# Row maxima turned pair by pair as seven 16-bit columns, with the bias product cut in four, in an attention and soft-MoE kernel

## The chip, the cores and the metric

The kernel runs on one core of one Trainium2 chip. The time is that of one execution on the device, in microseconds (us). The kernel before has a median of 298.84 us over three runs (298.15 to 299.03).

## The reference, cut to what matters

```python
# q, k, v: (8, 12, 448, 64) float32
scores = q @ k.T / 8
m = max(scores, axis=-1)
e = exp(scores - m)
attn = e / (sum(e, axis=-1) + exp(-m) + 1e-9)
x = (attn @ v), as 3584 rows of 768
logits = x @ phi                       # phi: 768 x 32
d = softmax of logits over the rows;   slot_input = d.T @ x
h = relu(slot_input[e] @ w1[e]);       slot_out[e] = h @ w2[e]     # 8 experts, 768x1024 and 1024x768
out = softmax of logits over the slots @ slot_out
```

## The kernel before, in words

**Pairs.** Two heads make a pair; there are 48 pairs (`NPAIR`), six to a batch element. Head 0 of a pair lies on partitions 0 to 63, head 1 on 64 to 127, so a product over the 64 channels of a head uses half of TensorE's rows, and the two heads' products can run side by side. The 448 queries are four blocks `i` of 128, 128, 128 and 64. For each pair the kernel does the following.

- `T(n)`, line 241: 28 transposes (L256) of 64x64 turn q and k; one copy takes the result from PSUM, on VectorE (L265) for two pairs in three, on ScalarE (L263) for the third. `NQK` = 7 turned pairs are kept.
- `A(n, i)`, line 274: scores of query block `i`, queries on the partitions (L285, L294, L304), into one of three PSUM buffers (`psA`), and VectorE's row maximum (L287, L298, L307). Seven maxima to a pair: two heads for each of the blocks 0 to 2, one for both heads of the half block 3.
- `W1`, `W2`, `W3`, lines 310 to 349: once for three pairs, GpSimd writes the negated maxima into a 128x4x128 tile `wm`, four matmuls turn it (L336, L337) into a row of 448 for each head and pair, ScalarE copies that as `mT` (L342), and two small exponentials give exp(-m) (L345, L348).
- `Bk(n, i)`, line 352: the scores again, keys on the partitions (L367 or L396), and onto them, in PSUM, the bias: the weights are a 0/1 column `sel` spread over the output's columns, the moving operand is `mT`, 448 wide (L370 or L399), one matmul for each head. ScalarE's exponential (L372, L402) reads the sum. Four PSUM buffers (`psB`), which `T`, `W2` and `PX` use too.
- `AV(n, i, qs)`, line 421: the product with v, 24 matmuls of 65 columns with 128-column weights and 8 with 64 columns (L436), into one PSUM buffer (`psV`); `N1` (ScalarE copy, L449) and `N2` (VectorE L464 and L465, GpSimd L469 to L480) divide by the sum; `PX` (L501, copy L507) turns the result.
- `P(b)`, line 516: after each batch element, the soft-MoE logits and their running sums, in steps spread over later half-pairs (`post`).

**The order is written out by hand.** Each engine works off its instructions in the order of the program. A string `ramp` (line 716) gives the order of the first pairs; then a loop (line 758) runs over the pairs `s` = 3 to 48, in two halves `y`. The list `runs` holds all `A(n, i)` in order (`i` = 0, 3, 1, 2 within a pair), and `As(c)` or a mixed `Bk` takes the next one from it. At `s` = 3, 26 of them have been taken: the maxima are (26 - 12)/4 = 3.5 pairs ahead. A half is *mixed* when the next `A` has `i` = 1 - `y` (line 761). A mixed `Bk` with `i` below 3 issues its matmuls as

```python
a0()         # A's head 0
score(1)
score(0)
bias(1)      # with its exponential
bias(0)
a1()         # A's head 1
```

so that the halves of the array hold (a0, score 1), (score 0, bias 1), (bias 0, a1). In the second half the block `i` = 3 of `Bk` follows with the `A` of `i` = 3 between its scores and its biases (`side`).

**Loads** all go out on GpSimd's queue (`load`, `load_part`), but for some of the last weight rows, which wait in DRAM in 16 bits and come by SyncE's queue (`stage_rows`, `fetch_rows`). `V(g)` (line 406, L408 to L411) is GpSimd's copy of v for three pairs, which waits for v's load. In the ramp, `G0` is `V(0)`, the load of v for group 1 and the fill of a buffer; `J0` is the load of q and k of group 2 and of a first weight half in two DMAs; `K0` is `V(1)`.

**The end.** After the last pair come the last `P`, the experts' products (`hidden` L862, `slots` L882) and the output (L925, sent at L941).

Of the kernel before, what the change touches and what calls it, by code (L numbers as in the profile page):

```python
# [8 lines left out]
F32 = mybir.dt.float32  # L9
# [22 lines left out]
def kernel(  # L32
# [39 lines left out]
    sel = const.tile([128, HG], BF16, name="sel")  # L72
    phi_sb = const.tile([128, KC, NS], BF16, name="phi_sb")
    halfm = const.tile([128, 2], F32, name="halfm")
    nhalfm = const.tile([128, 2], F32, name="nhalfm")
# [4 lines left out]
    NQK, NE, VPN, NATV = 7, 5, HG * 4 * VS, HG * 4 * D  # L80
    sizes = [("nq0", 2 * NP * S), ("nq1", 2 * NP * S), ("nv", NATV), ("qk6", 2 * S), ("wm1", 512),
             ("qk0", 2 * S), ("qk1", 2 * S), ("qk2", 2 * S), ("wm0", 512), ("xTa", 4 * 512), ("qk3", 2 * S),
             ("vp0", VPN), ("x0", 4 * DD), ("qk4", 2 * S), ("qk5", 2 * S), ("e2", NE * 2 * S), ("e1", S),
             ("vp1", VPN), ("xTb", 2 * 512), ("x1", 4 * DD)]
# [13 lines left out]
    wm = [part(f"wm{i}", 0, 512).rearrange("p (i c) -> p i c", i=4) for i in range(2)]  # L98
# [57 lines left out]

    with ExitStack() as at:
# [7 lines left out]
        nat = {}  # L165
        ubuf = pu.tile([128, 2, 7 * W65], F32, name="ubuf")
# [30 lines left out]
        for t in wm:  # L197
            nc.vector.memset(t, 0.0)
# [9 lines left out]
        for t, x in ((halfm, 1.0), (nhalfm, -1.0)):  # L208
            nc.vector.memset(t, 0.0)
            for hl in range(2):  # L210
                nc.vector.memset(t[64 - 64 * hl:128 - 64 * hl, hl:hl + 1], x)
# [10 lines left out]
        for base in (0, 64):  # L222

            nc.gpsimd.affine_select(
                out=sel[base:base + 64], in_=sel[base:base + 64], fill=1.0,
                compare_op=ALU.not_equal, base=0,
                pattern=[[-1, HG]], channel_multiplier=1)
# [3 lines left out]
        mx, ngm, ec, mT, eT, av, us = {}, {}, {}, {}, {}, {}, {}  # L231
# [9 lines left out]
        def T(n):  # L241
            g, pl = divmod(n, NP)
            first = n < NP * NP
# [26 lines left out]
        firsts = [0, 1] + list(range(3, NPAIR, 3))  # L270
        group = {n: (m, n - a) for m, (a, z) in enumerate(zip(firsts, firsts[1:] + [NPAIR])) for n in range(a, z)}
        mg, mpl = (lambda n: group[n][0]), (lambda m: (0, (firsts + [NPAIR])[m + 1] - firsts[m]))

        def A(n, i, steps=False):
            g, pl = group[n]
            if g not in mx:
                mx[g] = psm.tile([128, 21], F32, tag="mx", name="mx")
            t = qkT[n]
            if steps:
                m = mx[g]  # L280

                def run(hl):
                    r = slice(64 * hl, 64 * hl + 64)
                    ps = psA.tile([128, 512], F32, tag="a", name="ps_a")
                    nc.tensor.matmul(ps[:, 0:S], t[r, 0, i * 128:(i + 1) * 128], t[r, 1, :], start=True, stop=True)  # L285
                    c = HG * i + 2 * pl + hl
                    nc.vector.reduce_max(m[:, c:c + 1], ps[:, 0:S], axis=AX.X)  # L287

                return [lambda: run(0), lambda: run(1)]
            if i < 3:  # L290
# [5 lines left out]
                for hl in range(2):  # L296
                    c = HG * i + 2 * pl + hl
                    nc.vector.reduce_max(mx[g][:, c:c + 1], pss[hl][:, 0:S], axis=AX.X)  # L298
            else:
# [6 lines left out]
                c = 3 * HG + pl  # L306
                nc.vector.reduce_max(mx[g][:, c:c + 1], ps[:, 0:S], axis=AX.X)  # L307


        def W1(g):  # L310
            w, m = wm[g % 2], mx[g]
            l0, l1 = mpl(g)
            nm = psm.tile([128, 21], BF16, tag="ngm", name="ngm")
            neg = lambda o, s: nc.gpsimd.tensor_scalar(o, s, -1.0, None, op0=ALU.mult)
            cols = lambda t: t[:, 0:3 * HG].rearrange("p (i c) -> p i c", i=3)[:, :, 2 * l0:2 * l1]

            o = w[:, 3, :].rearrange("p (d c) -> p d c", d=2)[:, :, 2 * l0:2 * l1]
            nc.gpsimd.tensor_mul(
                o.rearrange("p d (l h) -> p d l h", h=2),
                m[:, 3 * HG + l0:3 * HG + l1].unsqueeze(1).unsqueeze(3).to_broadcast([128, 2, l1 - l0, 2]),  # L320
                nhalfm.unsqueeze(1).unsqueeze(1).to_broadcast([128, 2, l1 - l0, 2]))
            o = w[:, 0:3, :].rearrange("p i (d c) -> p i d c", d=2)[:, :, :, 2 * l0:2 * l1]
            neg(o, cols(m).unsqueeze(2).to_broadcast([128, 3, 2, 2 * (l1 - l0)]))
            if l1 - l0 == NP:
                neg(nm, m)
            else:
                nc.gpsimd.memset(nm, 0.0)
                neg(cols(nm), cols(m))
                neg(nm[:, 3 * HG + l0:3 * HG + l1], m[:, 3 * HG + l0:3 * HG + l1])
            ngm[g] = nm  # L330

        def W2(g):
            w = wm[g % 2]
            ps = pb_("ps_m")
            for i in range(3):
                nc.tensor.matmul(ps[:, i * 128:(i + 1) * 128], w[:, i, :], ident, start=True, stop=True)  # L336
            nc.tensor.matmul(ps[:, 384:448], w[:, 3, :], ident2[:, 0:64], start=True, stop=True)  # L337
            st["ps_m"] = ps

        def W3(g):  # L340
            t = psm.tile([128, S], BF16, tag="mT", name="mT")
            nc.scalar.copy(t, st["ps_m"][:, 0:S])  # L342
            mT[g] = t
            e = psm.tile([128, NP, 7], F32, tag="ec", name="ec", bufs=3)
            nc.scalar.activation(e[:, :, 0:6].rearrange("p l (i h) -> p i l h", i=3),  # L345
                                 ngm[g][:, 0:18].rearrange("p (i l h) -> p i l h", i=3, h=2),
                                 AF.Exp, scale=scale)
            nc.scalar.activation(e[:, :, 6], ngm[g][:, 18:21], AF.Exp, scale=scale)  # L348
            ec[g] = e


        def Bk(n, i, c=0, mix=False):

            g, pl = group[n]
            t = qkT[n]
            rs = [slice(0, 64), slice(64, 128)]
            if i < 3 and mix and runs and runs[0][1] < 3:
# [7 lines left out]
                def score(hl):  # L365
                    pss[hl] = pb_("ps_b")
                    nc.tensor.matmul(pss[hl][:, 0:S], t[rs[hl], 1, cols], t[rs[hl], 0, :], start=True, stop=False)  # L367

                def bias(hl):
                    nc.tensor.matmul(pss[hl][:, 0:S], sel[rs[hl], 2 * pl + hl:2 * pl + hl + 1].to_broadcast([64, 128]),  # L370
                                     mT[mg(n)][rs[hl], :], start=False, stop=True)
# [6 lines left out]
                bias(1)  # L378
                bias(0)
# [15 lines left out]
            for hl in range(2):  # L395
                nc.tensor.matmul(outs[hl], t[rs[hl], 1, cols], t[rs[hl], 0, :], start=True, stop=False)  # L396
            As(c)
            for hl in range(2):
                nc.tensor.matmul(outs[hl], sel[rs[hl], 2 * pl + hl:2 * pl + hl + 1].to_broadcast([64, m]), mT[mg(n)][rs[hl], :],  # L399
                                 start=False, stop=True)  # L400
# [14 lines left out]
        def av_tile(n):  # L415

            if n >= NPAIR - 3:
                return psA.tile([128, 512], F32, tag="a", name="ps_av")
# [22 lines left out]
        on_pool = lambda n: n < NPAIR - 4  # L441
# [10 lines left out]
        def N2(n):  # L452
# [5 lines left out]
            e = ec[mg(n)][:, group[n][1], :]  # L458
# [220 lines left out]
        for z in range(3):  # L679
            post.setdefault(2 * NPAIR - 5 + 2 * z, []).append(last[z])  # L680


        runs = [(n, i) for n in range(NPAIR) for i in (0, 3, 1, 2)]
# [8 lines left out]
        for _ in range(22):  # L692
            nc.tensor.matmul(ps[:, 0:64], wm[0][:, 0, :], wm[0][:, 0, 0:64], start=True, stop=True)
# [3 lines left out]
        rows_at = {77: 3, 83: 7, 85: 12, 89: 17, 91: 20, 92: 24, 93: 26, 95: 27}  # L697
        rows = 0
        stage_at = {34: [(16, 20), (20, 24)], 37: [(27, 29), (29, 32)], 40: [(32, 36), (36, 40)]}
        wait_loads = []  # L700
        waits = [r for z in stage_at.values() for y in z for r in range(*y)]
        def slot_loads(s):
            g = (s + 10) // 3
            if s == 1 or (s and s % 3 == 2):
# [4 lines left out]
            if s % 3 == 0 and g - 2 < NG - 1:  # L709
# [6 lines left out]
        ramp = ("T0 A A T1 A A W0 T2 A G0 A X0 J0 A B0.0 A B0.1 A A T3 A B0.2 A A T4 C0.3 V0.0 W1 A V0.1 V0.2 A X1 T5 "  # L716
                "A B1.0 A K0 V0.3 H0 C1.1 N0 B1.2 A T6 C1.3 V1.0 V1.1 A B2.0 M0 K1 A T7 B2.1 A V1.2 V1.3 W2 T8 H1 A "
                "N1 B2.2 Y2 V2.0 X2 C2.3 Z0 V2.1 M1 K2 ")
        for word in ramp.split():
# [7 lines left out]
            elif op == "W":  # L727
                W1(*arg)
            elif op == "X":
                W2(*arg)  # L730
                W3(*arg)
# [22 lines left out]
            elif op == "Z":  # L754
                PX(0)
            elif op == "K":
                slot_loads(*arg)
        for s in range(3, NPAIR + 1):
            for y in range(2):
                hs = 2 * s + y  # L760
                mix = len(runs) > 1 and runs[0][1] == 1 - y
# [17 lines left out]
                else:  # L779
                    if s < NPAIR - 6:  # L780
                        T(s + 6)
                    if s and s + 1 in firsts:
                        W2(mg(s + 1))
                        W3(mg(s + 1))
# [7 lines left out]
                if y == 0:  # L792
                    if 0 <= s - 1:
                        for i in range(4):
                            AV(s - 1, i, [3])
                        if s == NPAIR:
                            PX(s - 2)
                        N1(s - 1)
                        if not on_pool(s - 1):
# [4 lines left out]
                if y == 0 and s and s + 1 in firsts:  # L804
                    W1(mg(s + 1))
# [226 lines left out]
```

## Time and profile before

| | |
|---|---|
| median of three runs | 298.84 us (298.15 to 299.03) |
| span of the profiled execution | 298.99 us, printed as 299.0 |
| TensorE (PE) busy | 271.4 us, 91%, 5174 matmuls |
| VectorE (DVE) busy | 249.7 us, 84% |
| ScalarE (ACT) busy | 249.8 us, 84% |
| GpSimd (POOL) busy | 195.9 us, 66% |
| DMA | 58.67 MB, mean 196 GB/s |
| granted TensorE clock | full until the output stage |
| first exponential of pairs 0, 1, 2, 3, 4 | 12.75, 22.34, 27.16, 33.95, 38.62 us |
| first exponential of pairs 43 and 47, last of pair 47 | 229.05, 247.19, 250.1 us |

A line of the profile names the engine, the line of the kernel, the operation and its tiles: `L285 PE MATMUL ps_a<-W` is the matmul of line 285 that writes `ps_a`. PEld is the weight load of a matmul. "64\*128" is the part of the array used, rows by columns; "64x448" is the moving operand. The profiled execution spans 0.15 us more than the median of the runs, and nothing that the page shows lies around the span.

### The profile page before, as it was taken

The page shows a single profiled execution, that of the slowest core. Times are in us where ns is not written, and L with a number is a line of the kernel's source. Part 1 is how long each engine was busy: PE and PEld are TensorE (multiplying, and loading weights), DVE is VectorE, ACT ScalarE, POOL GpSimd, SP SyncE. Part 2 cuts the span into 40 slices and gives each one's busy share as a digit, 9 for nine tenths or more (in the row PEclk, how much of TensorE's full clock was granted, in tenths as well). Part 3 has the DMA queues.
Part 4 walks back from the last instruction along what each step waited for, and adds up shares of the span by engine and source line. Part 5 has one row for each costly group of instructions (what it writes and reads, how often), then busy time and mean ns, then how long its engine had stood idle before and what let it go on. Part 6 is the DMA issues. An engine that isn't in the chain of part 4 may idle for free.

```text
span 299.0 us, 12398 instructions
## 1 busy us (share of the span) xinstructions
PE 271.4 (91%) x5174; PEld 162.5 (54%) x5174; DVE 249.7 (84%) x581; ACT 249.8 (84%) x559; POOL 195.9 (66%) x391
## 2 busy tenths in 40 slices
PE   5999899999999999999899999999999999996820
PEld 4445456566666566566556666656665555652100
DVE  5899799999999989999889999998999675537930
ACT  3569999999899989998989899989999987337820
POOL 8792887979696979887879697978686633000000
PEclk9999999999999999999999999999999999997555
DMA  7999998999999999999999999999799989908997
GB/s 132 147 143 208 149 138 138 188 165 188 185 204 179 184 176 202 163 182 182 202 159 184 176 199 152 196 183 196 125 150 187 213 185 263 344 10 318 380 453 322
DMA packets 47015, 58.67 MB, mean 196 GB/s; under 512 B 2800, under 2 KB 39920, under 8 KB 46704
## 3 DMA queue, kind: packets, MB, share of 16 engines
q0 software_dynamic: 40304, 42.29, 89.6%
q1 hardware_dynamic: 6656, 15.60, 13.8%
q8 instruction: 40, 0.66, 0.8%
q14 instruction: 15, 0.12, 0.1%
HBM read 89.16 MB, written 15.14 MB: 349 GB/s over the span
## 4 chain that ended last, share of the span: by engine, by line
PE 68%; ACT 10%; DVE 6%; POOL 6%; issue 4%; DMA 2%; DVEq 0%; POOLq 0%; ACTq 0%
PE ps_av L436 15%; PE ps_a L285 10%; PE ps_b L367 7%; PE ps_b L370 7%; PE ps_t L256 5%; PE ps_b L396 5%; PE ps_x L501 3%; PE ps_b L399 3%; ACT W L402 2%; PE ps_o L925 2%; DVE mx L298 2%; PE ps_s L623 2%; PE ps_h L862 2%; PE ps_so L882 2%; ACT W L263 2%
## 5 line engine op out<-in xcount | busy, mean ns | idle before, releaser
L287 DVE TENSOR_REDUCE mx<-ps_a 128x1 f32<-128x448 f32 x250 | 137.3, 613 | 4.6 <-PE ps_a L285 3.5
L372 ACT ACTIVATE W<-ps_b 128x448 bf16<-128x448 f32 x250 | 120.4, 574 | 0.0
L285 PE MATMUL ps_a<-W 64*128 64x448 bf16 x250 | 80.9, 352 | 0.0
L367 PE MATMUL ps_b<-W 64*128 64x448 bf16 x250 | 70.5, 352 | 1.1
L436 PE MATMUL ps_av<-W 128*128 128x65 bf16 (+1 forms) x1536 | 64.9, 196 | 2.2 <-issue 1.6
L436 PEld LDWEIGHTS <-W 128*128 128x128 bf16 (+1 forms) x1536 | 50.5, 100 | 30.2 <-issue 26.4
L370 PE MATMUL ps_b<-mT,sel 64*128 64x448 bf16 x250 | 66.5, 350 | 0.0
L469 POOL TENSOR_TENSOR W<-ubuf,rec 128x384 bf16<-128x384 f32 x44 | 36.3, 824 | 35.7 <-ACT W L507 19.3
L402 ACT ACTIVATE W<-ps_b 128x448 bf16<-128x448 f32 x86 | 46.1, 574 | 2.0 <-PE ps_b L399 2.0
L256 PEld LDWEIGHTS <-W 64*64 64x64 bf16 x1344 | 29.3, 112 | 12.7 <-issue 4.3
L507 ACT CAST W<-ps_x 128x512 bf16<-128x512 f32 x47 | 28.6, 608 | 7.4 <-PE ps_x L501 7.2
L256 PE MATMUL ps_t<-ident,W 64*64 64x64 bf16 x1330 | 30.6, 195 | 2.4 <-ACT W L215 1.4
L307 DVE TENSOR_REDUCE mx<-ps_a 128x1 f32<-128x448 f32 x48 | 29.5, 615 | 1.4 <-PE ps_a L304 1.4
L285 PEld LDWEIGHTS <-W 64*128 64x128 bf16 x250 | 23.4, 94 | 9.8
L114 POOL DMA_DIRECT2D W<-in_moe_w_dram x30 | 22.6, 755 | 7.9 <-PE ps_b L399 7.8
L370 PEld LDWEIGHTS <-sel 64*128 64x128 bf16 x250 | 19.6, 94 | 14.4 <-issue 5.6
L396 PE MATMUL ps_b<-W 64*64 64x448 bf16 (+1 forms) x134 | 27.1, 374 | 0.3
L449 ACT COPY ubuf<-ps_av 128x455 f32<-128x455 f32 x44 | 25.1, 571 | 0.8 <-POOL W L408 0.6
L399 PE MATMUL ps_b<-mT,sel 64*64 64x448 bf16 (+1 forms) x134 | 25.1, 354 | 0.1
L263 ACT COPY W<-ps_t 128x896 bf16<-128x896 bf16 x21 | 19.5, 927 | 6.5 <-PE ps_t L256 6.5
L298 DVE TENSOR_REDUCE mx<-ps_a 128x1 f32<-128x448 f32 x38 | 21.1, 616 | 1.9 <-PE ps_a L294 1.9
L480 POOL TENSOR_TENSOR W<-ubuf,rec 128x128 bf16<-128x128 f32 x44 | 17.5, 398 | 3.7
(156 smaller groups left out, 446.6 us busy)
## 6 DMA issues: line engine op xcount, KB each, us to landing
W<-in_moe_w_dram POOLq DMA_DIRECT2D x24, 768.0 KB, 9.9
W<-in_v_dram POOLq DMA_DIRECT2D x32, 192.0 KB, 6.5
out_dram<-W SPq DMA_DIRECT2D x2, 2688.0 KB, 10.0
W<-in_q_dram POOLq DMA_DIRECT2D x15, 336.0 KB, 6.3
W<-in_k_dram POOLq DMA_DIRECT2D x15, 336.0 KB, 7.5
stage<-in_moe_w_dram POOLq DMA_DIRECT2D x4, 768.0 KB, 9.6
W<-stage SPq DMA_DIRECT2D x4, 576.0 KB, 7.3
out_dram<-W SPq DMA_DIRECT2D x6, 384.0 KB, 3.0
```

Of the source, the lines that this page charges most:

```text
L256: nc.tensor.transpose(o, src[r, pl, tok * D:(tok + 1) * D], ident[r, r])
L285: nc.tensor.matmul(ps[:, 0:S], t[r, 0, i * 128:(i + 1) * 128], t[r, 1, :], start=True, stop=True)
L287: nc.vector.reduce_max(m[:, c:c + 1], ps[:, 0:S], axis=AX.X)
L307: nc.vector.reduce_max(mx[g][:, c:c + 1], ps[:, 0:S], axis=AX.X)
L367: nc.tensor.matmul(pss[hl][:, 0:S], t[rs[hl], 1, cols], t[rs[hl], 0, :], start=True, stop=False)
L370: nc.tensor.matmul(pss[hl][:, 0:S], sel[rs[hl], 2 * pl + hl:2 * pl + hl + 1].to_broadcast([64, 128]), mT[mg(n)][rs[hl], :], start=False, s ...
L372: nc.scalar.activation(e[:, hl, :], pss[hl][:, 0:S], AF.Exp, scale=scale)
L396: nc.tensor.matmul(outs[hl], t[rs[hl], 1, cols], t[rs[hl], 0, :], start=True, stop=False)
L399: nc.tensor.matmul(outs[hl], sel[rs[hl], 2 * pl + hl:2 * pl + hl + 1].to_broadcast([64, m]), mT[mg(n)][rs[hl], :], start=False, stop=True)
L402: nc.scalar.activation(e, p[:, 0:S], AF.Exp, scale=scale)
L436: nc.tensor.matmul(o, eT[n, i, hl][:, qc], vp[g % 2][:, 2 * pl + hl, i, 0:W65], start=(i == 0 and u == 0 and hl == 0) or (u == 3 and i == ...
L469: eng.tensor_mul(x[:, 0:3, c:c + 128].rearrange("p i (h d) -> p i h d", h=2), u[:, 0:6, 0:D].rearrange("p (i h) d -> p i h d", h=2), rec[: ...
```

## The change

- The maxima of a pair are written by VectorE directly as seven 16-bit columns of a tile `mxr` (128 x 6 pairs x 64), not negated. `W1` on GpSimd, the tiles `wm`, `ngm` and `nhalfm` go.
- `W2(n)` runs for each pair: two transposes of 128x64 (one for each half of the output's partitions) and one ScalarE copy of 128x128 as `mT`. `EC` is one exponential for up to three pairs.
- `sel` holds -1, seven columns. The bias of a `Bk` is put on in four pieces of 128, 128, 128 and 64 columns for each head (`lower`): another column of `sel` for each piece, so 8 weight loads and 8 matmuls where there were 2 and 2.
- `NQK` = 5; `T` runs 4 pairs ahead in place of 6; the loads of q and k are issued at other places; a piece of the last weights gets room of its own (`own`).
- `runs` takes `i` in the order 0, 1, 3, 2; a half is mixed when the next `A` has `i` = 2 - `y`; the ramp is shorter and the loop begins at `s` = 2. In the ramp `J0` stands ahead of `G0`.

```diff
-    NQK, NE, VPN, NATV = 7, 5, HG * 4 * VS, HG * 4 * D
+    NQK, NE, VPN, NATV = 5, 5, HG * 4 * VS, HG * 4 * D
...
+        def W2(n):
+            ps = psB.tile([128, 128], BF16, tag="b", name="ps_m")
+            for r in rs:
+                nc.tensor.transpose(ps[r, :], mxr[:, n % (2 * NP), :], ident)
+            mT[n] = psm.tile([128, 128], BF16, tag="mT", name="mT", bufs=3)
+            nc.scalar.copy(mT[n], ps)
...
+        def lower(outs, n, m):
+            for i in range(4):
+                for hl, o in outs.items():
+                    c = 2 * i + hl if i < 3 else 6
+                    nc.tensor.matmul(o[:, i * 128:min(i * 128 + 128, S)], sel[rs[hl], c:c + 1].to_broadcast([64, m]),
+                                     mT[n][rs[hl], slice(0, 128) if i < 3 else rs[1 - hl]], start=False, stop=True,
+                                     skip_group_check=True)
...
                 a0()
                 score(1)
                 score(0)
-                bias(1)
-                bias(0)
+                lower({hl: pss[hl][:, 0:S] for hl in (1, 0)}, n, 128)
+                expo(1)
+                expo(0)
                 a1()
...
-            for hl in range(2):
-                nc.tensor.matmul(outs[hl], sel[rs[hl], 2 * pl + hl:2 * pl + hl + 1].to_broadcast([64, m]), mT[mg(n)][rs[hl], :],
-                                 start=False, stop=True)
+            lower(dict(enumerate(outs)), n, m)
...
-        runs = [(n, i) for n in range(NPAIR) for i in (0, 3, 1, 2)]
+        runs = [(n, i) for n in range(NPAIR) for i in (0, 1, 3, 2)]
...
-        ramp = ("T0 A A T1 A A W0 T2 A G0 A X0 J0 A B0.0 A B0.1 A A T3 A B0.2 A A T4 C0.3 V0.0 W1 A V0.1 V0.2 A X1 T5 "
-                "A B1.0 A K0 V0.3 H0 C1.1 N0 B1.2 A T6 C1.3 V1.0 V1.1 A B2.0 M0 K1 A T7 B2.1 A V1.2 V1.3 W2 T8 H1 A "
-                "N1 B2.2 Y2 V2.0 X2 C2.3 Z0 V2.1 M1 K2 ")
+        ramp = ("T0 A A T1 A A T2 A W0 J0 G0 A B0.0 A B0.1 T3 A B0.2 A C0.3 W1 T4 A V0.0 V0.1 A B1.0 V0.2 V0.3 H0 N0 A K0 "
+                "C1.1 T5 A B1.2 W2 A C1.3 E M0 K1 V1.0 V1.1 A Y ")
...
-        for s in range(3, NPAIR + 1):
+        for s in range(2, NPAIR + 1):
             for y in range(2):
                 hs = 2 * s + y
-                mix = len(runs) > 1 and runs[0][1] == 1 - y
+                mix = len(runs) > 1 and runs[0][1] == 2 - y
...
-                    if s < NPAIR - 6:
-                        T(s + 6)
-                    if s and s + 1 in firsts:
-                        W2(mg(s + 1))
-                        W3(mg(s + 1))
+                    if s < NPAIR - 4:
+                        T(s + 4)
...
+                        if s + 1 < NPAIR:
+                            W2(s + 1)
                         N1(s - 1)
+                        if s == 2 or s % 3 == 1 and s < NPAIR:
+                            EC(s - 1, s + 2 - (s == 2))
```

## The prediction

> **What bounds the kernel now.** I read the page's shares first, then the chain of waits, then the timeline of single pairs on each engine, and last GpSimd's queue at the start.
>
> ```profile
> PE 271.4 (91%) x5174; PEld 162.5 (54%) x5174; DVE 249.7 (84%) x581; ACT 249.8 (84%) x559; POOL 195.9 (66%) x391
> PE 68%; ACT 10%; DVE 6%; POOL 6%; issue 4%; DMA 2%; DVEq 0%; POOLq 0%; ACTq 0%
> ```
>
> TensorE (PE) carries 68% of the chain. A busy PE is not a PE at its peak, so I looked at the stretch that repeats, with the lines of ScalarE's copy L449, of which there is one for each pair:
>
> ```profile
> 40.00:200.00 160.00, 0.00 (x0) 18.91 (x33) 1.00 1.12 179
> ```
>
> 33 pairs in 160 us are 4.85 us a pair. More exactly: the first exponentials of pairs 4 and 43 start at 38.62 and 229.05 us, 39 pairs, **4.88 us a pair**. Now what each engine needs of that, by its starts back to back. VectorE: seven maxima 0.531 apart (3.72), two thirds of a 0.53 copy (0.35), the reciprocals (0.31), the soft-MoE steps (1.37 in six pairs, 0.23): 4.61. ScalarE: seven exponentials 0.424 apart (2.97), L449 0.43, L507 0.48, a third of a 0.786 copy (0.26), the turned maxima (0.64 in three pairs, 0.21), soft-MoE (0.12): 4.47. PE I read from the timeline of a pair, of which this is the later part:
>
> ```profile
> 181.09 0.54 PE L370 MATMUL ps_b<-mT,sel 64*128 64x448 bf16 x2
> 181.41 0.35 PE L285 MATMUL ps_a<-W 64*128 64x448 bf16 x1
> 181.69 0.54 PE L436 MATMUL ps_av<-W 128*128 128x65 bf16 x12
> 182.06 0.22 PE L582 MATMUL ps_bc<-ident,sm 128*128 128x128 bf16 x1
> 182.21 0.32 PE L436 MATMUL ps_av<-W 128*64 128x65 bf16 x8
> 182.47 0.35 PE L285 MATMUL ps_a<-W 64*128 64x448 bf16 x1
> 182.48 0.53 PE L367 MATMUL ps_b<-W 64*128 64x448 bf16 x2
> 182.68 0.52 PE L370 MATMUL ps_b<-mT,sel 64*128 64x448 bf16 x2
> 183.00 0.35 PE L285 MATMUL ps_a<-W 64*128 64x448 bf16 x1
> 183.28 0.38 PE L396 MATMUL ps_b<-W 64*64 64x448 bf16 x2
> 183.29 0.38 PE L304 MATMUL ps_a<-W 64*64 64x448 bf16 x2
> 183.49 0.35 PE L399 MATMUL ps_b<-mT,sel 64*64 64x448 bf16 x2
> 183.68 0.60 PE L256 MATMUL ps_t<-ident,W 64*64 64x64 bf16 x28
> 184.22 0.54 PE L436 MATMUL ps_av<-W 128*128 128x65 bf16 x12
> 184.59 0.38 PE L501 MATMUL ps_x<-ident,W 128*128 128x128 bf16 x4
> ```
>
> Read the starts, not the durations. Two 64-row matmuls of 448 columns, one in each half of the array, take a slot of 0.19 us (182.48 to 182.68). Where the tile's shape changes, PE first runs dry: L370's last matmul streams until 181.28, L285 until 181.60, and L436 starts at 181.69. That is 0.09 us for each change, some six to a pair: 41 changes from L285 to L396 between 20 and 240 us cost 3.67 us. In the same 45 pairs I summed by how much a matmul starts later than the one before it and the shape allow: 35 delays of 0.14 us at L285 after L370 (VectorE holds `psA`), 25 of 0.18 at L367 (ScalarE holds `psB`), a few single long ones, 16.4 us in all, 0.36 a pair. So PE needs 4.88 - 0.36 = **4.52 us**. Three engines need 4.5 to 4.6 us of 4.88: what is added to PE beyond 0.36 must lengthen the pair, and what is added below it may.
>
> **The order that the change really makes.** The ramp of the changed program takes 18 `A` (15 words A, 3 words C) before `s` = 2: that is (18 - 8)/4 = 2.5 pairs ahead, not 1.75. The next one has `i` = 3, and each half takes two, so the first half always meets `i` = 3 and the second `i` = 0. The new condition wants 2 and 1: **no half is mixed any more**, and the instruction order of the built program shows this for every pair. PE per pair is now: A3 | scores, pieces, scores, pieces, A2 | AV, AV of the half block, W2 | A0, scores, pieces | scores 3, pieces | A1 | T | AV, PX.
>
> **PE, step by step, per pair.**
> - Slots: before 3+3 in the first half, 3 in the second, then the scores of block 3 together with A3 in one of 0.21 (183.28 to 183.49), then a bias: 11. Now A3 has a slot of its own: 12. +0.17.
> - Shape changes: before 64x128, 128x128, 128x64, 64x128, 64x64, 128x128: six. Now A3 (64x64) stands ahead of 64x128, and A1 (64x128) between two 64x64: nine. +3 x 0.09 = +0.27. (A change from 64x64 to 64x128 is in the trace at the start alone, 0.096.)
> - Pieces: no row has 64x128 weights with 128 columns. The nearest are L501 (128 columns, a weight load each, four in 0.22: 0.055) and L256 (64x64 in both halves, 28 in 0.445: 0.032 a pair of them). Both heads' pieces then take 3 x 0.055 + 0.032 = 0.197 where the uncut bias took 0.19: +0.03 in four blocks. From below: the columns are the same, so no gain. From above: every pair of pieces waits for its own weight load, 0.094 (row below): 4 x 0.094 = 0.376, +0.74. I take +0.03, by L501 and L256, whose loads hide behind shorter matmuls.
>
> ```profile
> L370 PEld LDWEIGHTS <-sel 64*128 64x128 bf16 x250 | 19.6, 94 | 14.4 <-issue 5.6
> ```
>
> - `W2`: two transposes side by side, 0.06, in the shape of the AV ahead of it. It was 0.27 for three pairs: -0.03.
>
> Sum +0.44: PE needs 4.96 us, VectorE and ScalarE what they did. (ScalarE: 128 columns lie between the rows of 18 and of 448, 0.12 and 0.43, so some 0.20 a pair for `mT` and 0.04 for `EC`, against 0.21; the 16-bit output of the maximum I take as free, since the 448 inputs stay.) Now PE is alone at the top. Of the 0.36 of waits I keep 0.12: those at `psA` go, since the `A` now come in pairs a microsecond apart, about what VectorE takes for two, while those at `psB` come in the third of the pairs whose `T` copy is ScalarE's, and there stay in part. **A pair takes 5.08, +0.20**; over 42.5 pairs (`s` = 3 until the last `A`) +8.5 us. Without any wait +0.08 (3.4 us), with all of them +0.44 (18.7).
>
> One page rates the pieces dearer. The Trainium skill, "TensorE: Matmul & The Clock Gate", section "Back-to-back issue gap", gives about 81 ns for each matmul in a stream of weight loads and 128-column matmuls. By it a pair would cost 4 x (4 x 0.081 - 0.197) = 0.51 us more, and the sum would be about 330; the 0.055 of L501 speaks against it, on a full array.
>
> **The start.** GpSimd's timeline before, with the v load of group 1 ahead of the weight half:
>
> ```profile
> 13.75 0.67 POOL L181 DMA_DIRECT2D W<-in_v_dram  x1
> 16.69 0.77 POOL L176 DMA_DIRECT2D W<-in_q_dram  x1 [0.40 <-ACT W L402]
> 18.23 1.54 POOL L114 DMA_DIRECT2D W<-in_moe_w_dram  x2
> 20.84 0.67 POOL L408 COPY W<-W 128x576 bf16<-128x576 bf16 x1
> ```
>
> That load landed at 17.85, so `V(1)` at 20.84 waited for nothing. Now `J0` goes first. Landings come in the order of issue: k of group 1 at 14.77, phi 15.20; q and k of a group take 2.74 each, the weight DMAs 3.65 and 3.83, v twice 1.0. So v lands at 15.2 + 5.5 + 7.5 + 2 = 30.2. `V(1)` stands on GpSimd ahead of the division of pair 0, and takes 2.0 us, the division 1.6: 33.8. PE's queue holds `PX(0)` at the end of `s` = 2. PE would be there at 29.7: the 20 maxima after `T3`, which waits for k of group 1, run from 15.4 to 26.0, and PE goes on two to three buffers ahead, so `s` = 2 starts at 25.2 and takes 4.5. PE stands for 4 us, with all that is queued behind it. `s` = 3 then has its first exponential at 34.6, before 33.95: **+0.7**, where a shorter ramp alone would have given -3.4. This eats what the shorter lead gains.
>
> **The end.** With 2.5 pairs ahead in place of 3.5, one pair less runs without `A`; before, such pairs took 4.5 (229.05 to 247.19: four in 18.1). +0.4. The last weights landed at 262.85 and are used from 264.2 on; both move along with the pairs. `W1` goes from GpSimd, 0.81 in three pairs; its 66% wait for others anyhow: 0.
>
> **Sum.** 299.0 + 8.5 + 0.7 + 0.4 = **308.6 us**. The span is 0.15 above the median of the runs; I leave that out.
>
> **Rivals.**
> - *The waits stay.* If the 0.36 are lag between engines that a longer PE does not take up, a pair takes 5.32: 299.0 + 18.7 + 1.1 = 318.8. For it: they are there with three engines at 92 to 94%. Against: VectorE and ScalarE now have 0.35 to 0.5 us to spare. Chance 0.12 (above 315).
> - *Weight loads not hidden*, as above: +0.74 x 44 = 33, some 341, or 330 halfway. The alternating 64x64 loads of L256 speak against it. Chance 0.07.
> - *Faster: the three added shape changes don't drain PE.* Then PE needs 4.69, the evenly spaced `A` take the waits at `psA` away, and VectorE's 4.61 is next: a pair takes 4.70, 299.0 - 7.7 + 1.1 = 292.4. It decides if less than 0.33 of the 0.44 are real. For it: the change from 128x128 to 128x64 costs only 0.06. Against: 41 changes from 64x128 to 64x64 at 0.09. With the wait for `V(1)` gone as well it would be 289. Chance 0.13.
> - *Nearly nothing*: no waits left, and v lands 2 us earlier: 299 + 3.4 - 1.3 + 0.4 = 301.5, or less by some of the next. Chance 0.10, of which 0.04 within 0.3%.
>
> **The numbers.** The forecast, 302 to 315, has 0.58. The range goes from 300.5 to 320: it holds the forecast, the waits that stay, and part of the last rival. 0.3% (0.9 us) is about what a measurement of this kernel can tell from no change. Faster 0.13, same 0.04, slower 0.83.
>
> **What would show it.** In the profile after: PE without a mixed half, nine shape changes to a pair at 0.09; pieces 0.055 apart for both heads (0.09 would be the weight loads); pairs 5.0 to 5.2 apart; GpSimd's `V(1)` waiting for a DMA until 30, and PE for GpSimd at L471 (`PX`) near 30 to 34. It would be wrong if pairs are 4.9 or less apart, or if PE's added matmuls find it waiting anyhow.

## The result and the profile after

The changed kernel takes **322.14 us** (320.25 to 323.37), the kernel before 298.50 beside it: a ratio of 1.077 (95% interval 1.072 to 1.082), slower. The forecast was 308.6, the range 300.5 to 320.0: right in sign, outside the range. Medians are over all runs of a kernel; the ratios leave out the slow runs (one of e5, two of e13).

The engines' busy time and the shares of the chain of waits, from the page of the kernel after:

```profile
PE 293.8 (92%) x6354; PEld 200.7 (63%) x6354; DVE 257.5 (80%) x574; ACT 252.7 (79%) x573; POOL 184.4 (58%) x340
...
PE 77%; ACT 8%; DVE 4%; DMA 3%; issue 3%; POOL 1%; DVEq 0%; ACTq 0%; POOLq 0%
```

TensorE (PE) was 68% of the chain and is 77%; ScalarE's share fell from 10% to 8%, GpSimd's from 6% to 1%. So PE is alone at the top, as forecast. The stretch that repeats, by ScalarE's copy of `ps_av` (now L419), 40 to 200 us:

```profile
40.00:200.00 160.00, 0.00 (x0) 17.13 (x30) 1.00 1.04 165
```

30 pairs where there were 33. By first exponentials, pair 4 starts at 37.90 (before 38.62), pair 43 at 248.42 (229.05): **5.40 us a pair**, before 4.88. Of the 21.1 us by which the span grew, 39 pairs hold 20.1; the start gives back 0.7, and 1.7 come behind pair 43.

One pair of PE after, between two starts of `A3` (line 296), with parts left out:

```profile
148.77 0.38 PE L296 MATMUL ps_a<-W 64*64 64x448 bf16 x2
149.08 0.36 PE L367 MATMUL ps_b<-W 64*128 64x448 bf16 x2
149.28 0.36 PE L320 MATMUL ps_b<-mT,sel 64*128 64x128 bf16 x8
149.48 0.39 PE L367 MATMUL ps_b<-W 64*128 64x448 bf16 x2
...
150.80 0.22 PE L304 MATMUL ps_m<-ident,mxr 128*64 128x128 bf16 x2
150.95 0.36 PE L287 MATMUL ps_a<-W 64*128 64x448 bf16 x2
...
151.85 0.36 PE L320 MATMUL ps_b<-mT,sel 64*64 64x128 bf16 x8
152.14 0.36 PE L287 MATMUL ps_a<-W 64*128 64x448 bf16 x2
152.43 0.63 PE L254 MATMUL ps_t<-ident,W 64*64 64x64 bf16 x28
...
153.68 0.38 PE L296 MATMUL ps_a<-W 64*64 64x448 bf16 x2
```

Read the starts again. Eight pieces take 0.20 us (149.28 to 149.48), as much as the slot of the uncut bias did. `A3` has a slot of its own: 148.77 to 149.08 is 0.21 and a change of shape. `A1` (152.14) stands between two 64x64 forms. Nothing waits here, and the pair still takes 4.91; the mean of 5.40 holds the soft-MoE steps and the waits too.

For every run I made the same account of PE, from the trace's records between the first exponentials of pairs 4 and 43. The columns of a matmul are counted as 0.187 us for 448, an estimate from the slots of 0.19. A gap behind them of up to 0.125 us (counted from 0.06) is a change of shape; a longer one is a wait, by its releaser; what is left is work. "Issue" is a gap with no releaser.

| us a pair | pair | work | changes of shape (number) | waits for engines | issue | matmuls | median, us |
|---|---|---|---|---|---|---|---|
| before | 4.88 | 4.10 | 0.58 (6.2) | 0.12 | 0.08 | 97 | 298.5 |
| **after** | 5.40 | 4.35 | 0.88 (9.1) | 0.10 | 0.07 | 122 | 322.1 |
| e3: after, uncut | 5.28 | 4.33 | 0.88 (9.2) | 0.07 | 0 | 98 | 315.8 |
| e1: lead 1.75 | 5.34 | 4.21 | 0.58 (6.2) | 0.14 | 0.40 | 122 | 320.2 |
| e2: e1, unmixed | 5.26 | 4.23 | 0.59 (6.3) | 0.23 | 0.21 | 122 | 317.5 |
| e8: e1, pieces by head | 5.29 | 4.19 | 0.59 (6.2) | 0.16 | 0.35 | 122 | 318.8 |
| e9: e2, uncut | 5.07 | 4.22 | 0.60 (6.4) | 0.25 | 0.01 | 98 | 307.4 |
| e10: e1, uncut | 4.94 | 4.15 | 0.59 (6.4) | 0.18 | 0.02 | 98 | 302.1 |
| e14: e1, zero weights | 5.34 | 4.18 | 0.59 (6.3) | 0.18 | 0.38 | 122 | 318.3 |
| e15: e14, two pieces | 4.96 | 4.16 | 0.59 (6.3) | 0.18 | 0.03 | 106 | 302.7 |
| e4: before, unmixed | 5.02 | 4.22 | 0.60 (6.4) | 0.20 | 0 | 97 | 306.3 |
| e5: before, cut | 5.25 | 4.17 | 0.60 (6.3) | 0.09 | 0.39 | 121 | 317.4 |

### The profile page after: what moved, and what is told of

It reads as the page before. It is cut to its first block, busy times and chain, and to the rows that moved or that the text cites. A ratio compares the mean times of both kernels' runs of the same rounds, so it can differ in the third digit from the quotient of the medians.

```text
span 320.1 us, 14666 instructions
## 1 busy us (share of the span) xinstructions
PE 293.8 (92%) x6354; PEld 200.7 (63%) x6354; DVE 257.5 (80%) x574; ACT 252.7 (79%) x573; POOL 184.4 (58%) x340
## 4 chain that ended last, share of the span: by engine, by line
PE 77%; ACT 8%; DVE 4%; DMA 3%; issue 3%; POOL 1%; DVEq 0%; ACTq 0%; POOLq 0%
PE ps_av L406 15%; PE ps_b L367 14%; PE ps_a L287 12%; PE ps_b L320 11%; PE ps_t L254 7%; PE ps_a L296 4%; ACT W L372 4%; PE ps_x L471 3%; DVE mxr L290 3%; DMA W<-in_k_dram 3%; PE ps_o L880 2%; PE ps_s L593 2%; PE ps_h L817 2%; PE ps_l L505 2%; PE ps_so L837 2%
## 5 line engine op out<-in xcount | busy, mean ns | idle before, releaser
L290 DVE TENSOR_REDUCE mxr<-ps_a 128x1 bf16<-128x448 f32 x288 | 165.0, 621 | 21.4 <-PE ps_a L287 17.4
L372 ACT ACTIVATE W<-ps_b 128x448 bf16<-128x448 f32 x336 | 158.8, 564 | 14.9 <-PE ps_b L320 13.3
L320 PEld LDWEIGHTS <-sel 64*128 64x128 bf16 (+1 forms) x1536 | 65.1, 98 | 24.8 <-issue 7.3
L367 PE MATMUL ps_b<-W 64*128 64x448 bf16 (+1 forms) x384 | 77.4, 362 | 1.0 <-ACT W L477 0.5
L320 PE MATMUL ps_b<-mT,sel 64*128 64x128 bf16 (+3 forms) x1536 | 76.1, 211 | 0.9 <-issue 0.9
L287 PE MATMUL ps_a<-W 64*128 64x448 bf16 x288 | 60.8, 366 | 1.6 <-DVE mxr L290 0.7
L298 DVE TENSOR_REDUCE mxr<-ps_a 128x1 bf16<-128x448 f32 x48 | 28.7, 598 | 3.0 <-PE ps_a L296 1.4
L367 PEld LDWEIGHTS <-W 64*128 64x128 bf16 (+1 forms) x384 | 19.3, 96 | 16.9 <-issue 12.7
L419 ACT COPY ubuf<-ps_av 128x455 f32<-128x455 f32 x45 | 26.1, 580 | 0.0
L471 PE MATMUL ps_x<-ident,W 128*128 128x128 bf16 x192 | 18.9, 219 | 1.2 <-issue 1.0
L296 PE MATMUL ps_a<-W 64*64 64x448 bf16 x96 | 18.5, 381 | 0.2 <-DVE mxr L290 0.2
L378 POOL COPY W<-W 128x576 bf16<-128x576 bf16 x16 | 10.6, 664 | 12.3 <-DMA W<-in_v_dram 9.9
```

Source lines behind the costliest of these rows:

```text
L287: nc.tensor.matmul(pss[hl][:, 0:S], t[r, 0, i * 128:(i + 1) * 128], t[r, 1, :], start=True, stop=True)
L290: nc.vector.reduce_max(mcol(n, i, hl), pss[hl][:, 0:S], axis=AX.X)
L296: nc.tensor.matmul(ps[64 - 64 * hl:128 - 64 * hl, 0:S], t[r, 0, 384:448], t[r, 1, :], start=True, stop=True)
L298: nc.vector.reduce_max(mcol(n, 3), ps[:, 0:S], axis=AX.X)
L320: nc.tensor.matmul(o[:, i * 128:min(i * 128 + 128, S)], sel[rs[hl], c:c + 1].to_broadcast([64, m]), mT[n][rs[hl], slice(0, 128) if i < 3 e ...
L372: nc.scalar.activation(e, p[:, 0:S], AF.Exp, scale=scale)
```

## The experiments

The theory after the result (A): the order that the ramp really makes, 2.5 pairs ahead with nothing mixed, costs PE a slot and three changes of shape, while the pieces are nearly free. The rivals: the pieces themselves cost; the shorter lead and the turn in every pair hold PE through `psB`.

### First round: the order, and the pieces

**e1**, three maxima fewer in the ramp: a lead of 1.75 pairs, at which the condition of the change does mix the halves:

```diff
-                "C1.1 T5 A B1.2 W2 A C1.3 E M0 K1 V1.0 V1.1 A Y ")
+                "B1.1 T5 A B1.2 W2 A B1.3 E M0 K1 V1.0 V1.1 Y ")
```

> The changed kernel with three maxima less taken in the ramp (15 in place of 18), so that the lead is 1.75 pairs and every half is mixed. Main theory (the order costs TensorE a slot and three shape changes a pair): these come back, 0.17 + 0.3, but a mixed half with alternating pieces puts the two halves of the array out of step, +0.35 a pair by slots of 0.19 us: 5.1 to 5.25 us a pair in place of 5.40, 308 to 316 us. Rival one (the pieces and their weight loads are the cost): unchanged, 319 to 324. Rival two (the short lead makes engines wait): slower than 322.

**e2**, the same with `mix = False`, so that no half is mixed:

> As the kernel with 15 maxima in the ramp, but no half mixed: both heads of an A stand together, and the A of the half block shares a slot with the scores of the half block. Main theory: six shape changes and eleven slots as before the change, no step lost by the pieces: 4.85 to 5.0 us a pair, 296 to 304 us. Rival one (the pieces are the cost): 319 to 324. Rival two (the short lead makes engines wait): above 312.

**e8**, e1 with the pieces of a mixed half sorted by head:

```diff
+            order = [(i, hl) for i in range(4) for hl in outs]
+            if by_head:
+                order.sort(key=lambda z: -z[1])
...
```

> As the kernel with 15 maxima in the ramp and mixed halves, but in a mixed block the four pieces of head 1 come first and then the four of head 0, so that the pairs (a0, score 1), (score 0, pieces 1), (pieces 0, a1) are kept. Main theory: 4.85 to 5.0 us a pair, 296 to 304 us, some 10 us below the one with alternating pieces. Rival one (the pieces are the cost in any order): within 3 us of the one with alternating pieces.

**e3**, the order of after, the bias uncut. Its weights are zero columns, so it leaves the maxima on the scores and waits for no turned maximum:

```diff
-            for i in range(4):
...
+            t = qkT[n]
+            for hl, o in outs.items():
+                nc.tensor.matmul(o, mxr[rs[hl], 0, 63:64].to_broadcast([64, m]), t[rs[hl], 0, :], start=False, stop=True,
+                                 skip_group_check=True)
```

> The changed kernel in its own order, with one bias product of 448 columns for each head and block in place of four pieces; its weights are zero columns, so the maxima are not taken off the scores. Main theory: the pieces are nearly free, 0.03 us a pair: 318 to 322 us. Rival one (the pieces and their weight loads are the cost): 300 to 305.

Measured: e1 320.23 (ratio 1.071, 1.067 to 1.076), e2 317.53 (1.062, 1.058 to 1.067), e8 318.83 (1.066, 1.060 to 1.072), e3 315.82 (1.056, 1.053 to 1.060). All four missed what theory A expected; e1 and e8 came where the rival of the pieces had them, e2 only where that of the short lead did, e3 in neither range. Sorted by head (e8), the pieces cost what they do alternating: the intervals of e1 and e8 overlap. The mended order does what it was to do to PE (changes of shape from 0.88 back to 0.58, work from 4.35 to 4.2), and yet a pair takes 5.26 to 5.34. What came in its place is seen in PE's waits of e1, 38 to 228 us (us in total, times, longest):

```profile
PE ps_t L254 <- issue: 4.8, 6, 1.4
PE ps_av L406 <- issue: 2.3, 4, 1.0
PE ps_b L338 <- issue: 1.6, 1, 1.6
```

PE stands for up to 2 us with no engine and no data transfer to release it, at any line. (This list counts from a matmul's modelled end; counted from the end of its columns, over the 39 pairs, there is more.) e3, where PE is as slow as in after and has 98 matmuls a pair, has none of this. Number the matmuls of the trace from 0: of 21 such gaps in e1, 17 (15.0 of 15.8 us) end at a matmul whose number leaves **95 when divided by 128**; in e2 it is 10 of 10, in before 4 of 4, in after 6 of 6, in e5 below 18 of 22. 128 matmuls and their 128 weight loads are 256 instructions, and the instruction queue q8 moves packets of 16,384 bytes, 64 for each. PE waits for its own instructions. From here on, theory A is that this is what the pieces cost.

### Second round: both undone, and the parts put into the kernel before

**e9** is e2 with the uncut bias of e3 (zero weights), **e10** is e1 with it.

> Both undone at once: 15 A in the ramp (1.75 pairs ahead, block 3's maximum shares its slot with the scores of block 3, 11 slots, six changes of shape) and the bias uncut, as one product of zero weights (the maxima are not taken off). What theory A says (the pieces cost little as long as PE is slow, but their 2360 further PE instructions are fetched too late when PE gets faster): PE needs about what it did before, no idle time of PE ends by itself at matmul 95 of 128, a pair takes 4.8 to 4.95, and the kernel takes 296 to 302 us. The rival (the short lead and the turn of the maxima in every pair hold PE through psB, whatever the pieces do): the two gains only add up, 298.6 + (317.5 - 298.6) - 6 = 311, and 308 to 313 would show it.

> As the run before, but with the halves mixed as the diff's condition wants them (the two halves of the array change between maxima and scores). The bias is one product of zero weights, the maxima are not taken off. Theory A: within 2 us of that run, 296 to 302. The rival (psB and the short lead): 308 to 313. If mixing itself is worth something, this run is the faster of the two by more than 2 us.

**e4** is the kernel before with `mix = False`.

> The kernel before with mix = False alone: block 3's maximum still shares its slot with the scores of block 3, so it keeps 11 slots, six changes of shape and 3.5 pairs of lead. Main theory (the extra slot and the three changes of shape cost, not the lost mixing): 297 to 301. The rival (mixing spreads the maxima, and without it VectorE holds psA): 303 to 310.

**e5** is the kernel before with its bias cut:

```diff
...
+            for i in range(4):
+                for hl, o in outs.items():
+                    z = slice(i * 128, min(i * 128 + 128, S))
+                    nc.tensor.matmul(o[:, z], sel[rs2[hl], 2 * pl + hl:2 * pl + hl + 1].to_broadcast([64, m]),
+                                     mT[mg(n)][rs2[hl], z], start=False, stop=True, skip_group_check=True)
...
```

> The kernel before, its bias in four pieces that alternate between the heads, all else as it was (the same columns, 1232 more matmuls each with its weight load). Theory A (fetch of PE's instructions): stalls of PE once in 128 matmuls, 306 to 316. The rival (pieces are nearly free, +0.03 a pair and a shifted slot in the mixed halves): 299 to 304.

Measured: e9 307.39 (1.028, 1.025 to 1.031), e10 302.12 (1.012, 1.008 to 1.016), e4 306.32 (1.026, 1.023 to 1.028), e5 317.44 (1.060, 1.055 to 1.065). Of theory A's ranges, e10 and e5 lie just above (by 0.1 and 1.4 us), e9 and e4 by over 5; e4 is in its rival's range.

*The pieces.* Cutting the bias alone costs the kernel before 6.0%, some 18 us. Of its +0.37 a pair, 0.31 are "issue", 0.07 work, changes of shape 0.02, and waits for engines fell by 0.03. In the mended order (e10 to e1) it is +0.40, of which issue 0.38. In after's order (e3 to after) it is +0.12, issue 0.07. Here is one such gap on e5's timeline:

```profile
121.31 0.38 PE L406 MATMUL ps_b<-W 64*64 64x448 bf16 x2
121.32 0.37 PE L304 MATMUL ps_a<-W 64*64 64x448 bf16 x1
122.58 0.35 PE L304 MATMUL ps_a<-W 64*64 64x448 bf16 x1 [0.89 <-issue]
122.58 0.38 PE L357 MATMUL ps_b<-mT,sel 64*64 64x128 bf16 x8
```

The first matmul of L304 ran at 121.32, its twin for the other half of the array, which needs nothing that the first did not, at 122.58: matmul 2655 = 20 x 128 + 95. And what the DMA queues moved from 120.2 to 121.3 us:

```profile
q8 instruction: 1, 0.02, 5.5%
```

That packet (120.27 to 121.25 us) ended 1.33 us before matmul 2655 began. In nine kernels (before, after, e1, e2, e3, e5, e10, e14, e15) I set the packets against these matmuls, one by one, the first packet with matmul 223. There is one packet to every 128 matmuls (40, 43 or 49 in all), and none of the matmuls starts earlier than 1.14 us after its packet landed. Each one that PE stood for (over 0.125 us, between 40 and 230 us) starts 1.2 to 1.6 us after the landing, so it is the late packets that PE waits for.

*The mixing.* e4 is 7.3 us slower than before, and e9 5.3 slower than e10; my theory gave the mixing nothing. The rival of e4 (VectorE holds `psA`) has a part: waits for engines rise by 0.08 (e4) and 0.07 (e9), and VectorE releases 0.06 and 0.10 a pair, where in before and e10 it releases none. The rest shows in a stretch of e4's timeline:

```profile
183.82 0.53 PE L396 MATMUL ps_b<-W 64*128 64x448 bf16 x2
184.01 0.53 PE L399 MATMUL ps_b<-mT,sel 64*128 64x448 bf16 x2
184.21 0.52 PE L294 MATMUL ps_a<-W 64*128 64x448 bf16 x2
184.66 0.54 PE L436 MATMUL ps_av<-W 128*128 128x65 bf16 x12
```

A pair of matmuls side by side spans 0.36 (as at 152.14 above); here the two heads run 0.18 apart, and the row of slots ends that much later (184.21 to 184.66 is 0.45; 152.14 to 152.43 above, the same slot and a change of shape as long, 0.29). One half of the array idles while the other runs, and my account calls that work: 4.10 to 4.22, with the same matmuls and columns. Why mixed halves escape it is argued only: their order is staggered from the start, and the last maximum fills the end.

### Third round: another way to an uncut bias, and the lead

**e11** is e1 with true maxima, which are turned into a row of 448 columns:

```diff
+            for i in range(4):
+                for hl in range(2):
+                    o, x = (slice(i * 128, i * 128 + 128), ident) if i < 3 else (slice(384, 448), ident[:, rs[1 - hl]])
+                    nc.tensor.matmul(ps[rs[hl], o], mcol(n, i, hl).to_broadcast([128, 64]), x, start=True, stop=True)
...
```

> Pair by pair as in the change, 1.75 pairs ahead and mixed, and the whole result computed, but each pair's maxima are turned into one row of 448 columns a head (eight matmuls with the maximum's column as weights, in place of two transposes), so that the bias is one product again. 103 matmuls a pair in place of 121. Theory A (what the pieces cost is the number of PE instructions, and little else): the 302.1 of the uncut run with zero weights, plus at most 0.15 a pair for six more matmuls and something for ScalarE's copy of 448 columns in place of 128: 303 to 309, without stalls at matmul 95 of 128. The rival (the uncut runs were fast because their weights were zero, or because no maxima were turned into them in time): 313 to 320.

**e12** and **e13** add a word A to the ramp of after (19 `A`: 2.75 pairs ahead, and mixed), the one with the row, the other with the uncut bias of zero weights.

> As the run before with one pair more of lead (19 A in the ramp, 2.75 pairs ahead; five turned pairs suffice for it). If the short lead holds PE (a maximum that comes late for W2): 1 to 4 us below that run. If the lead only shifts work between ramp and tail: within 1.5 us of it.

> The uncut run with zero weights (the maxima are not taken off), mixed, with 2.75 pairs of lead in place of 1.75. That run took 302.1, 3 us over the kernel before. If the lead is what is left of the difference: 299 to 300.5. If not (the turn in every pair and its buffer of psB): 301 to 304.

Measured: e11 313.79 (1.050, 1.044 to 1.055), e12 314.41 (1.053, 1.046 to 1.059), e13 302.27 (1.010, 1.006 to 1.013). The lead does nothing: e12 against e11, and e13 against e10, are equal within their spread, so the rival of the short lead falls. e11 has no issue gaps to speak of (0.01 a pair), but missed theory A's range and lies by number in the rival's. Its pair is 5.14, 0.20 over e10: work 0.16 (eight turning matmuls take 0.19 on its timeline, two transposes took 0.05), waits for engines 0.03. The other 4 us of its 11.7 over e10 lie outside the 39 pairs. That left the doubt whether zero weights made e3, e9 and e10 fast.

### Fourth round: is it the count?

**e14** is e1 with zero weights in four pieces, **e15** with two:

```diff
+            for a, z in ((0, 256), (256, S)):
+                for hl, o in outs.items():
+                    nc.tensor.matmul(o[:, a:z], mxr[rs[hl], 0, 63:64].to_broadcast([64, m]), t[rs[hl], 0, a:z], start=False,
+                                     stop=True, skip_group_check=True)
```

> The 1.75-ahead, mixed order with the bias in four alternating pieces, as in its first run (320.2), but the pieces have the zero weights and the moving rows of the uncut run (302.1); the maxima are not taken off. Theory A (it is the number of PE instructions): 317 to 322, with stalls at matmul 95 of 128. The rival (zero weights, or no wait for the turned maxima, made the uncut runs fast): 302 to 308.

> The same with two pieces a head in place of four (256 and 192 columns, zero weights, the maxima are not taken off): some 105 matmuls a pair in place of 121 or 97. If a packet of 128 matmuls comes every 5.9 us at the least where PE waits for it, 105 matmuls in 4.97 us ask for one in 6.06, and only dense stretches wait: 302 to 306, a third of the pieces' cost or less, with 5 us of such stalls at most. The rival (each piece costs the same, by its weight load or its place between the heads): 302.1 + 18.1/3 = 308, and 307 to 310 would show it.

Measured: e14 318.26 (1.062, 1.055 to 1.069), e15 302.69 (1.012, 1.005 to 1.018). Instruction queue and chain, first of e14, then of e15:

```profile
q8 instruction: 49, 0.80, 1.0%
...
PE 62%; ACT 14%; issue 8%; DVE 5%; DMA 5%; POOL 3%; DVEq 0%; ACTq 0%; POOLq 0%
```

```profile
q8 instruction: 43, 0.70, 0.9%
...
PE 61%; ACT 15%; DMA 7%; POOL 5%; DVE 4%; issue 4%; DVEq 0%; ACTq 0%; POOLq 0%
```

With zero weights the four pieces cost the same as with true ones, so the data is not it. And the cost does not grow piece by piece: two pieces cost 0.6 us over one (e10), within the spread, four 16.1. Both runs lie in the ranges of theory A. At 106 matmuls a pair and 4.96 us, 128 matmuls take 6.0 us; at 122 and the 5.0 us that PE would need, 5.2 us, and they get 5.6. It is a rate that sets in, not a price.

No version here beats the kernel before. A true bias in two pieces was not tried.

## Why the prediction was wrong

- **The bound, the order and the sign: right.** PE is alone at the top, no half is mixed, there are 9.1 changes of shape to a pair (forecast nine). e3 to e10 shows what the order costs: 13.7 us with the bias uncut.
- **Slots, pieces and `W2`: +0.17 forecast, +0.25 measured.** The slot of `A3` adds 0.21, not 0.17. PE's time for the pieces is what the row of L501 said (0.02 to 0.03 a pair, e3 against after), and the two transposes take about 0.05 (150.80 to 150.95, less a change of shape). Some 0.04 is left that no run separates; as no half is mixed, the slip that e4 shows may be in it. The rival of weight loads that aren't hidden is false as a mechanism: 0.20 us for eight pieces leaves 25 ns for each. The 81 ns of the Trainium skill, "TensorE: Matmul & The Clock Gate", section "Back-to-back issue gap", do not hold for this 64-row form with two heads side by side. (The rival's "330 halfway" should read 325: 308.6 and half of 33.)
- **Changes of shape: +0.27 forecast, +0.30 measured** (0.097 each in after).
- **The waits: -0.24 forecast, -0.03 measured. This is the step that failed:** "Of the 0.36 of waits I keep 0.12". The 0.36 was a sum of lateness, not of waits: a matmul can start late while the other half of the array still streams, and my account leaves that in the work. By gaps of PE, before has 0.12 for engines, none of it for VectorE, and 0.08 for instructions, so PE's need was 4.68 and not 4.52. And of the 0.20, 0.17 are there after the change: ScalarE's share fell, but some for VectorE came (0.04), and the wait for instructions stayed although PE is slower, since it has a quarter more of them (e3, with 98 matmuls a pair in the same order, has none). Together: forecast +0.20, measured +0.52, times 39 pairs the 20.1 us. The rival "the waits stay" (318.8, chance 0.12) came nearest and was right that they stay; but only part of what stayed is lag between engines, and its sum was short by the two small terms above.
- **The start: +0.7 forecast, -0.7 measured.** GpSimd's timeline of after, and PE's:

```profile
27.85 0.66 POOL L378 COPY W<-W 128x576 bf16<-128x576 bf16 x1 [9.94 <-DMA W<-in_v_dram]
```

```profile
31.51 0.39 PE L471 MATMUL ps_x<-ident,W 128*128 128x128 bf16 x4
```

`V(1)` does wait 9.9 us for the load, as forecast, but v landed at 27.70, not 30.2: behind phi (14.71), q and k of group 2 took 1.65 and 1.73 us where I had 2.74 each. GpSimd ends the division at 31.48 (31.08 + 0.40), and PE comes to `PX(0)` just then (31.51, I had 29.7), so nobody stood.
- The rivals on the fast side are false: the added changes of shape do drain PE, and the waits did not all go. The 0.06 that I gave for the change from 128x128 to 128x64 was a misreading; in before its median is 0.097 (39 of them).
- **Behind pair 43: +1.1 forecast** (3.5 pairs at 0.20, and 0.4)**, +1.7 measured.**
- What I did not see at all: the mixing has a worth of its own (5 to 7 us), and the pieces' 1200 matmuls bring PE to the rate at which its instructions arrive. In after the second costs less (some 6 us, e3 against after), because its order had already made PE slow: the causes are not a sum. With the uncut bias of zero weights the mended order is 20 us faster than after (e10, 302.1); with the pieces it is 2 (e1, 320.2).
- Open: on what the arrival of a packet depends (between 40 and 230 us its transfer begins from 0.5 us before to 4.4 us after the matmul 95 ahead of it, and I found no rule); and the 3 us that e10 lies over before, of which 0.06 a pair are waits for ScalarE, mostly.

## What to carry to other kernels

Count instructions, not only columns: where matmuls are cut, work out how long 128 of them take, and set it beside the time at which the instruction queue's packets land. Look where "issue" gaps fall in the count of instructions before you call them noise. And before waits are booked as a reserve that new work will use up, count only gaps with a named releaser, and ask for each whether the change takes away what releases it.

## What the runs showed of the hardware

- PE's instructions arrive in packets of 16,384 bytes (256 instructions), one to 128 matmuls and their weight loads, and a packet is used at the earliest 1.14 us after it landed. Where PE could do 128 matmuls in 6.0 us (e15) or 6.3 to 6.4 (before, e10), the waits are 0.02 to 0.08 us a pair; in 5.6 (after) 0.07, in 5.3 (e2) 0.21, in 5.2 (e1, e14) 0.38 to 0.40. The Trainium skill, "Runtime: NRT & Kernel Launch", section "Instruction fetch mechanics", gives the same block, 16 KiB or 256 instructions, and calls the cost of crossing it mostly hidden, since instructions are issued more slowly than they are filled. The block agrees with these runs; that it is hidden holds in before (3.2 us) and not in e5 (15.2 us).
- Eight 64-row pieces (for each head three of 128 columns and one of 64), each with its own weights, take the 0.20 us of two matmuls of 448 when two heads alternate.
- A half of the array that waits while the other works shows as busy PE (e4: 0.12 us a pair more work by my account than in before, with the same matmuls).
- A change of the tile's shape costs PE about 0.1 us: 9.1 of them a pair cost 0.88 in after, 6.2 cost 0.58 in before.
